# Two-sided attention on one core: six-slot bursts up to the last scores, the segment units' P @ V and the maxima's transposition later, the third octet earlier

## The chip, the cores and the metric

The kernel runs on one core of one Trainium2 chip. The metric is the device time of one execution, in microseconds (us). The engines of the core run side by side, each through its own list of instructions in order, and wait for each other by semaphores: TensorE (PE in the profile) multiplies matrices into PSUM, VectorE (DVE) and ScalarE (ACT) read PSUM, GpSimd (POOL) works on SBUF, and SyncE (SP) issues most of the DMA transfers. PSUM has eight banks of 128 partitions by 512 fp32 values, and one matrix product fills at most one bank.

## The reference

Two attentions over the same input x (2048 rows, 512 columns) are mixed by a gate, in fp32:

```python
g = sigmoid((x * gate_w).sum(-1, keepdims=True))
a = A(x)   # 32 heads of 16, softmax(q k^T / 4) v over all 2048 keys, then @ A_wo
b = B(x)   # 32 heads of 16, four segments of 512 rows:
           #   a_dot = causal softmax inside the segment, times v
           #   a_mem = (phi(q) M) / (phi(q) z + 1e-6), from the segments before
           #   o = gB * a_mem + (1 - gB) * a_dot, then @ B_wo
           #   M, z += the segment's phi(k)^T v and the sum of phi(k)
return g * a + (1 - g) * b
```

phi(t) is t + 1 for t > 0 and exp(t) otherwise; gB is the sigmoid of one number a head.

## The kernel before, in words

**Front part.** Projections of q, k and v for both sides, the gate, and B's memory terms. An fp32 value that goes into a product is split into a rounded high part and the rest (low), and three products stand for one. q and k are stored so that one product over 48 rows does all three terms of a score.

**Units and slots.** The main part is a list of units (side, g, c): four heads (group g of 8) and 512 query rows (chunk c of 4). A unit of side A has 64 slots, a unit of side B (a "segment unit") 10. One slot is one score tile: `score_part` issues the product of 128 keys by 512 queries into a PSUM bank (L661), and one exponential on ACT from there into the tile `p` (L684, L681). Four slots share a `p` tile, and there are six of these (`NP`). Units A and B alternate; the last two are B (group 7, chunk 3) and A (group 7, chunk 3). There are nS = 2368 slots in all, and the last A unit begins at slot 2304.

**Maxima ahead.** The exponent needs each row's maximum. `max_part` computes it 96 slots (`LEAD`) ahead of the scores: a product into one of four banks `sm` (L200) and a reduction on DVE (L215; L225 for the masked tiles of B). So the last 96 slots have none, and from slot 2272 on the four `sm` banks are free for other things. After a unit's last maximum, `finish_max` reduces on DVE (L178) and splits the result on POOL into `ms` (L182, L183). A number of slots later (`LATE_T` for A, four more for B) `run_late` transposes `ms` on PE into a bank `mt_ps` of the pool `st` (L191), ACT copies it to `mt` (L194), and SP writes it into two spare rows of the unit's q (L197). From then on the score product subtracts the maximum by itself. `run_late` is looked at only at the end of a burst, and takes up to two units at once.

**Bursts.** PE changes between three kinds of work: scores and maxima, P @ V, and output products. It is given them in bursts: three slots (`BURST`), then the P @ V of what is old enough. In the range `wide` (slots 2274 to 2333) a burst is six slots, the first three with the `st` banks and the next three with the free banks `sm1` to `sm3`.

**P @ V.** A piece is 128 query columns of four heads, done as four products side by side (17 columns of v each, the last one counting the sum). When a `p` tile is complete, its four pieces enter `queue` with the slot from which they may run (`GAP`, or six slots in the wide range); `some_values` joins neighbours of the same tile (L717). All go into one bank `ops`; at a unit's end ACT copies it to `oraw` (L721) and SP stores it to `od` (L722). A tile of a segment unit is first masked on POOL, by one or two `affine_select` (L665).

**Octets.** Two groups of one side make an octet of eight heads. `octet` schedules, at fixed distances in slots from t0, six steps: load (SP), factors (POOL: a reciprocal by `pow`, L776, and five small operations), send (SP: the factors to DRAM, L785), factor (SP: them back, broadcast, L789), scale (POOL, L792 to L801), store (SP, `hd`, L809). POOL and SP take these in program order, between the other things that they are given: SP the transposed maxima (L197), loads of k and v, stores; POOL the splitting of the maxima and the masks.

**Output products.** Each 128 rows of the output are 24 products (four octets, two sides, three products each, L822). Those of the chunk before are done between units. The last ones are a list `fill`, in this order: 24 for the last block of chunk 2 (bank `sm0`), 18 for block 0 of chunk 3 (`sm0` again, octets 0 to 2), and 66 for what is left except A's last octet. `load_closed` fetches the scaled octets for them (L900). In the wide range four are issued a burst, behind it two a burst of three slots. Behind the last unit's `oraw`, A's last octet is done with DVE in place of POOL, and its 12 products and the copies to the output end the kernel.

**What sets the order.** The loop at the end of `gated_mix` runs over slots n. In each it runs what is filed under `beside[n]` (octet steps, loads), then the score, the maximum of slot n + 96, and at a burst's end P @ V and either a transposition or output products.

Of the kernel before, what the change touches and what calls it, by code (L numbers as in the profile page):

```python
# [23 lines left out]
NCH = S // CH  # L24
KT = D // 128
NG = 8
# [8 lines left out]
LEAD = 96  # L35
BURST = 3
# [1 line left out]
LOW, HIGH = 6, 14  # L38
NP = 6
GAP = {"A": 2, "B": 5}  # L40
LATE_T = 8
PRE = 20
NKA, NKB = 8, 2

# [2 lines left out]
def gated_mix(ctx, tc, x, xT, wqkv, a_wo, b_wq, b_wk, b_wv, b_wo, beta, gate_w, out):  # L47
# [59 lines left out]
    end = {u: first[u] + SLOTS[u[0]] for u in units}  # L107
    seg_end = {(s, c): max(end[s, g, c] for g in range(NG)) for s in "AB" for c in range(NCH)}
    nS = len(slots)
# [4 lines left out]
    for k in range(NU):  # L114
# [4 lines left out]
        for p in range(64 + 10 * len(bs)):  # L119
            r = (len(maxs) + 1) % 2  # L120
            i = (p - start) // apart
# [42 lines left out]
    def rows(t, h, n):  # L164

        return t[64 * (h // 2):64 * (h // 2) + n, h % 2]
# [7 lines left out]
    def finish_max(u):  # L174
        nm = pmt.pop(u)
        if u[0] == "A":
            pm, nm = nm, mp.tile([128, 4, 4], F32, tag="nm", name="nm")
            nc.vector.tensor_reduce(nm, pm, axis=AX.X, op=ALU.max, negate=True)  # L178

        ms = mp.tile([128, 2, 2, 2, 4], F32R, tag="ms", name="ms")  # L180
        nv = nm.rearrange("p (r h) s -> p r h s", r=2)
        nc.gpsimd.tensor_copy(ms[:, :, 0], nv)  # L182
        nc.gpsimd.tensor_sub(ms[:, :, 1], nv, ms[:, :, 0].bitcast(F32))  # L183
        return ms
# [18 lines left out]
    def max_part(m, bank):  # L203
# [24 lines left out]
        if m == last_max[u]:  # L228
            def finish():
                late.append((m + LATE_T + (4 if side == "B" else 0), u, finish_max(u)))  # L230
            todo.append((m, finish))
# [29 lines left out]
    with ExitStack() as p0:  # L261
# [136 lines left out]
        early = vp.tile([128, NG, 4, 4, 17], F32, tag="vs", name="vs").rearrange("p g b h e -> p (g b h e)")  # L398
        early = [early[:, 1024 * i:1024 * i + 1024] for i in range(2)]
# [238 lines left out]
    stored = set()  # L638


    wide = range(nS - LEAD + 2, nS - 34)
    assert wide.start % (2 * BURST) == wide.stop % (2 * BURST) == 0

    queue = []

    def score_part(n):

        u, j = slots[n]
        side, g, c = u
        q = qt[u]  # L650

        if j % 4 == 0:
            pt_[u, j // 4] = pp.tile([128, 4, CH], F32, tag="p", name="p")
            order_p[u, j // 4] = len(order_p)
            assert not queue or order_p[queue[0][1], queue[0][2] // 4] > len(order_p) - 1 - NP
        p = pt_[u, j // 4]
        h = (0, 2, 1, 3)[j % 4]

        def score(ps, h, b, k, n0, q0):

            nc.tensor.matmul(ps[:, n0:n0 + CH - q0], rows(k[:, :, b * 128:(b + 1) * 128], h, 50),  # L661
                             rows(q[:, :, q0:], h, 50), start=True, stop=True)

        def diagonal(x):
            nc.gpsimd.affine_select(out=x, in_=x, pattern=[[0, 4], [1, 128]], base=0, channel_multiplier=-1,  # L665
                                    compare_op=ALU.is_ge, fill=0.0)

        ps = banks[1 + n % BURST] if n in wide and n // BURST % 2 else st_ps.tile([128, CH], F32, tag="st", name="st")
        if side == "A":
            score(ps, h, j // 4 % 4, kt_[u, j // 16], 0, 0)  # L670
        else:
            k = kt_[u, c]
            if j < 8:
                score(ps, h, j // 4, k, 0, 128 * (j // 4))
                if j >= 4:
                    score(ps, h, 3, k, 384, 384)
            else:
                for f in range(2):
                    score(ps, 2 * (j - 8) + f, 2, k, 256 * f, 256)
        if side == "B" and j >= 8:  # L680
            nc.scalar.activation(p[:, 2 * (j - 8):2 * (j - 8) + 2, 0:256], ps.rearrange("p (h t) -> p h t", h=2), AF.Exp,  # L681
                                 scale=SCALE)
        else:
            nc.scalar.activation(p[:, h], ps, AF.Exp, scale=SCALE)  # L684
        if j % 4 == 3 or j == SLOTS[side] - 1:
            if side == "B":
                diagonal(p[:, :, 0:128])
                if j == 7:
                    diagonal(p[:, :, 384:])
            queue.extend((n + (2 * BURST if n in wide else GAP[side]), u, i) for i in range(j // 4 * 4, j + 1))  # L690


    PIECES = ([(0, 128 * i, 128 * i) for i in range(4)] + [(1, 128 * i, 128 + 128 * i) for i in range(3)] + [(3, 384, 384)]
# [2 lines left out]
    def some_values(n, most):  # L696

        while queue and most and queue[0][0] <= n:
            _, u, i = queue.pop(0)
            most -= 1  # L700
            side, g, c = u
            w = 1
            while (queue and most and queue[0][0] <= n and queue[0][1] == u and (i + w) // 4 == i // 4
                   and (side == "A" or PIECES[i + w][0] == PIECES[i][0])):
                queue.pop(0)
                most -= 1
                w += 1
            p = pt_[u, i // 4]
            if side == "A":
                c0 = q0 = 128 * (i % 4)  # L710
                v = vt[u][:, i // 16, i // 4 % 4]
            else:
                b, c0, q0 = PIECES[i]
                v = vt[u][:, b]
            done = i + w == SLOTS[side]
            for h in range(4):
                nc.tensor.matmul(ops[32 * h:32 * h + 17, q0:q0 + 128 * w], v[:, 17 * h:17 * h + 17], p[:, h, c0:c0 + 128 * w],  # L717
                                 start=(i == 0), stop=done, tile_position=(0, 32 * h))
            if done:
                raw = ob.tile([128, CH], F32, tag="o", name="oraw")  # L720
                nc.scalar.copy(raw, ops)  # L721
                nc.sync.dma_start(od[side, c][4 * g:4 * g + 4].rearrange("h r t -> (h r) t"), raw)  # L722
                stored.add(u)
                if side == "B" and c and g % 2 == 0:
                    octet("M", g // 2, c, n + 4)
                if (side, g ^ 1, c) in stored and u != ("A", NG - 1, NCH - 1):
                    octet(side, g // 2, c, n + (20 if side == "B" and u != ("B", NG - 1, NCH - 1) else 8))
                if u in between:
                    shared.extend(output(*between[u]))
                return  # L730
# [19 lines left out]
    def octet(side, o, c, t0, vector=False):  # L750
# [6 lines left out]
        ending = o == NO - 1 and c == NCH - 1  # L757
# [51 lines left out]
                nc.sync.dma_start(hd[side, c][o], raw(k["hl"]))  # L809
                scaled.add((side, o, c))  # L810

        ts = (0, 10, 14, 18, 28, 28) if ending else (0, 10, 25, 29, 42, 54)
        for n, f in zip(ts, (load, factors, send, factor, scale, store)):
            if t0 is None:
                f()
# [3 lines left out]
    def products(ps, t, b, side, o, start, stop):  # L819

        for i, (x, w) in enumerate(((1, 0), (0, 1), (0, 0))):
            yield lambda i=i, x=x, w=w: nc.tensor.matmul(ps, t[:, b, x], wos[side][:, o, w], start=start and i == 0,  # L822
                                                         stop=stop and i == 2)
# [49 lines left out]
    last = NCH - 1  # L873
# [30 lines left out]
    def close(n, side, o, b):  # L904
        for i in range(3):
            def f(i=i):
                assert (side, o, last) in scaled
                list(products(banks[b], closed[side, o], b, side, o, (side, o) == closing[0], (side, o) == closing[-1]))[i]()
            fill.append((n, f))
    early = [(k, 0) for k in closing[:6]]  # L910
    for (side, o), b in early + [(k, b) for k in closing[:-1] for b in range(4) if (k, b) not in early]:
        close(nS - 66 if ((side, o), b) in early else max(nS - 12, end[side, 2 * o + 1, last] + 60), side, o, b)

    def jam(n):

# [5 lines left out]
    n = 0  # L921
    while n < nS or queue or beside or filled[0] < len(fill):
        for f in beside.pop(n, []):
            f()
        if n < nS:
            score_part(n)
        m = n + LEAD
        if m < nS:
            loads(m + PRE)

            max_part(m, lambda: banks[m % 4])
        run_todo(m)
        if n >= nS or n % (2 * BURST if n in wide else BURST) == (2 * BURST if n in wide else BURST) - 1:
            if shared:
                for _ in range(4):
                    shared.pop(0)()
            else:
                some_values(n, 8 if n >= nS or n in wide else MOST + jam(n))
            if n < 5:


                for i in range(4):
                    nc.tensor.matmul(ops[:, 128 * i:128 * i + 128], identf, identf, start=True, stop=True)
            if any(e[0] < m + 1 for e in late):
                run_late(st_ps, "st", m + 1)
            else:
                for _ in range(4 if n in wide else 2 if n < nS else 0 if queue else 4):
                    if filled[0] == len(fill) or fill[filled[0]][0] > n:
                        break
                    fill[filled[0]][1]()  # L950
                    filled[0] += 1
        n += 1
# [45 lines left out]
```

## Time and profile before

| | |
|---|---|
| three runs | 1836.19 us median (1835.84 to 1837.24) |
| the profiled execution | 1836.33 us, of which its span is 1834.1 us |
| PE, DVE, ACT, POOL busy | 1816.6, 1586.7, 1450.3, 605.0 us |
| mean granted TensorE clock | 0.999 |

The profile shows one execution. Its page gives each engine's busy time, the span in 40 slices, the DMA queues, the chain of work that ended last, and the costliest groups of instructions. Other views used here: the busy time of each engine in chosen stretches of the span (windows), who waited for whom (waits), and instructions in order of time, merged where neighbours are alike (timeline: start, duration, engine, line, operation, output and inputs, count, and in brackets the idle time before and what ended it). PE's matmuls overlap, so the time from one group's start to the next group's start says more than a duration. A product of fp32 operands appears as two records.

### The profile page before, as it was taken

To read this page: it belongs to the slowest core of one execution; us is meant where nothing else is said; L and a number is where in the kernel's file an instruction comes from. 1 tells how busy PE (TensorE), PEld (TensorE's weight loads), DVE (VectorE), ACT (ScalarE), POOL (GpSimd) and SP (SyncE) were. 2 spreads that over 40 slices of the span, in tenths; PEclk is the share of its full clock that TensorE was granted. 3 is DMA by queue.
4 is the path that set the end of the run, shared out by engine and by line. 5 is a ranking of instruction groups with operands and counts; after the bars stand their busy time and mean duration, and the time that the engine had idled before them with its cause. 6 is when DMAs were issued, how large, how long until landed. Compare 5 with 4: busy or idle time off the path is not lost.

```text
span 1834.1 us, 41634 instructions
## 1 busy us (share of the span) xinstructions
PE 1816.6 (99%) x15473; PEld 974.7 (53%) x15473; DVE 1586.7 (87%) x3333; ACT 1450.3 (79%) x2768; POOL 605.0 (33%) x708
## 2 busy tenths in 40 slices
PE   9999999999999999999999999999999999999998
PEld 7887766545545555444444444444444444444444
DVE  4234677999999999999999999999999999999910
ACT  5445444788888888888888888888888888888884
POOL 3001222234141414334433434342424342525351
PEclk9999999999999999999999999999999999999999
DMA  6568645433334334445454545454545444444441
GB/s 225 201 216 266 210 175 181 150 114 108 118 107 120 106 117 120 141 124 142 124 142 124 142 124 142 124 141 124 141 124 142 124 138 107 146 120 129 134 153 48
DMA packets 140617, 258.46 MB, mean 141 GB/s; under 512 B 36184, under 2 KB 60280, under 8 KB 139904
## 3 DMA queue, kind: packets, MB, share of 16 engines
q1 hardware_dynamic: 138912, 254.15, 46.7%
q8 instruction: 123, 2.02, 0.5%
q0 software_dynamic: 1216, 1.14, 0.2%
q14 instruction: 78, 0.64, 0.1%
q10 hardware_dynamic: 288, 0.52, 0.1%
HBM read 171.25 MB, written 83.25 MB: 139 GB/s over the span
## 4 chain that ended last, share of the span: by engine, by line
PE 88%; DVE 5%; POOL 2%; ACT 2%; DMA 1%; issue 1%; SPq 0%; POOLq 0%; DVEq 0%; ACTq 0%
PE ops L717 30%; PE st L661 26%; PE sm L200 13%; PE pr L298 12%; DVE pm L215 4%; PE ops L822 4%; PE sm L822 2%; POOL rcp L776 1%; DVE rest L225 1%; POOL mn L358 1%; PE num L480 1%; ACT p L684 0%; DMA raw<-xT 0%; PE mt_ps L191 0%; DMA raw<-wqkv 0%
## 5 line engine op out<-in xcount | busy, mean ns | idle before, releaser
L684 ACT ACTIVATE p<-st 128x512 f32<-128x512 f32 x2276 | 1198.6, 601 | 176.2 <-PE sm L200 118.0
L215 DVE TENSOR_REDUCE pm<-sm 128x1 f32<-128x512 f32 x2048 | 1262.1, 683 | 13.9 <-PE sm L200 13.7
L200 PE MATMUL sm<-kA,qA 48*128 48x512 f32 x2048 | 734.7, 445 | 0.0
L661 PE MATMUL st<-qA,kA 50*128 50x512 f32 x2029 | 670.2, 433 | 1.2 <-ACT mt L194 0.9
L717 PE MATMUL ops<-p,vA 128*17 128x256 f32 (+3 forms) x7440 | 560.6, 404 | 0.0
L661 PEld LDWEIGHTS st<-qA,kA 50*128 50x128 f32 x2029 | 329.8, 185 | 393.2 <-ACT p L684 332.1
L200 PEld LDWEIGHTS sm<-kA,qA 48*128 48x128 f32 x2048 | 333.6, 184 | 24.3 <-DVE pm L215 7.9
L776 POOL TENSOR_TENSOR rcp<-rec,minus 128x32 f32<-128x32 f32 x43 | 234.3, 5448 | 112.6 <-DMA rec<-dend 78.5
L717 PEld LDWEIGHTS ops<-p,vA 128*17 128x17 f32 x7440 | 153.8, 96 | 201.6 <-issue 159.4
L225 DVE CUSTOM_DVE_ANT_0 rest<-sm,mask 128x128 f32<-128x128 f32 (+3 forms) x512 | 248.6, 486 | 6.8
L665 POOL TENSOR_SCALAR_AFFINE_SELECT p<-p 128x512 f32<-128x512 f32 x128 | 79.5, 640 | 343.6 <-ACT p L684 328.3
L200 PE MATMUL sm<-kB,qB 48*128 48x128 f32 (+3 forms) x512 | 149.0, 351 | 0.0
L361 DVE TENSOR_TENSOR q<-full,q 128x512 fp32r<-128x512 f32 x64 | 44.5, 695 | 87.1 <-ACT q L354 87.1
L661 PE MATMUL st<-qB,kB 50*128 50x512 f32 (+1 forms) x495 | 109.4, 334 | 0.9 <-ACT p L684 0.8
L182 POOL CAST ms<-pm 128x16 fp32r<-128x16 f32 x32 | 6.3, 198 | 303.8 <-DVE pm L225 303.8
L661 PEld LDWEIGHTS st<-qB,kB 50*128 50x128 f32 x495 | 70.0, 185 | 61.1 <-ACT p L684 54.9
L200 PEld LDWEIGHTS sm<-kB,qB 48*128 48x128 f32 x512 | 86.9, 185 | 6.7 <-DVE pm L215 2.7
L717 PE MATMUL ops<-p,vB 128*17 128x512 f32 (+3 forms) x1024 | 87.2, 437 | 1.9 <-POOL p L665 1.9
L353 ACT COPY full<-pr 128x512 f32<-128x512 f32 x64 | 37.4, 584 | 51.1 <-PE pr L298 50.9
L358 POOL TENSOR_SCALAR mn<-full 128x512 f32<-128x512 f32 x24 | 36.3, 1512 | 102.1 <-ACT full L353 81.7
L772 DVE RECIPROCAL rec<-rec 128x32 f32<-128x32 f32 x1 | 0.4, 354 | 67.0 <-DMA rec<-odA 67.0
L298 PE MATMUL pr<-xh,wql 128*128 128x512 f32 x128 | 54.5, 426 | 1.9 <-ACT xh L411 1.7
(178 smaller groups left out, 1575.3 us busy)
## 6 DMA issues: line engine op xcount, KB each, us to landing
kA<-kdA SPq DMA_DIRECT2D x256, 128.0 KB
vA<-vdA SPq DMA_DIRECT2D x31, 544.0 KB
kA<-kdA SPq DMA_DIRECT2D x256, 64.0 KB
qdA<-q SPq DMA_DIRECT2D x32, 256.0 KB
kdA<-q SPq DMA_DIRECT2D x32, 256.0 KB
qdB<-q SPq DMA_DIRECT2D x32, 256.0 KB
qA<-qdA SPq DMA_DIRECT2D x64, 128.0 KB
kdB<-q SPq DMA_DIRECT2D x32, 256.0 KB
```

The costliest lines, as they stand in the source:

```text
L200: nc.tensor.matmul(ps[:, n0:n0 + n], rows(qt[u][:, :, s * 128:(s + 1) * 128], h, 48), rows(k[:, :, k0:k0 + n], h, 48), start=True, stop=True)
L215: nc.vector.tensor_reduce(pm[:, h, s, kc:kc + 1], ps, axis=AX.X, op=ALU.max)
L225: nc.vector.tensor_tensor_reduce(out=tri["rest"][:, 0:w], in0=ps[:, n0:n0 + w], in1=tri["mask"][:, CH - w:], scale=-1.0, scalar=3.0e38, op ...
L298: nc.tensor.matmul(ps, l(a, k), r(b, k), start=(n == 0), stop=(n == 11))
L358: nc.gpsimd.tensor_scalar_min(ph["mn"], full, 0.0)
L361: nc.vector.tensor_sub(q2, full, q1.bitcast(F32))
L661: nc.tensor.matmul(ps[:, n0:n0 + CH - q0], rows(k[:, :, b * 128:(b + 1) * 128], h, 50), rows(q[:, :, q0:], h, 50), start=True, stop=True)
L665: nc.gpsimd.affine_select(out=x, in_=x, pattern=[[0, 4], [1, 128]], base=0, channel_multiplier=-1, compare_op=ALU.is_ge, fill=0.0)
L684: nc.scalar.activation(p[:, h], ps, AF.Exp, scale=SCALE)
L717: nc.tensor.matmul(ops[32 * h:32 * h + 17, q0:q0 + 128 * w], v[:, 17 * h:17 * h + 17], p[:, h, c0:c0 + 128 * w], start=(i == 0), stop=done ...
L776: eng.tensor_tensor(r, rec, minus, op=ALU.pow)
L822: yield lambda i=i, x=x, w=w: nc.tensor.matmul(ps, t[:, b, x], wos[side][:, o, w], start=start and i == 0, stop=stop and i == 2)
```

## The change

Six edits. `LATE_T` goes from 8 to 10. The wide range ends at slot 2363 in place of 2333. In the wide range a segment unit's pieces may run after twelve slots, not six. The octets of heads 16 to 23 in chunk 3 (the third, of sides A and B and of B's memory term) get shorter distances, and B's begins 8 slots behind its unit's last P @ V, not 20. The closing products behind the first 18 may be issued from slot nS, not nS - 12. And output products come in fours wherever they come, except while P @ V is still queued behind the last slot.

```diff
-LATE_T = 8
+LATE_T = 10
...
-    wide = range(nS - LEAD + 2, nS - 34)
+    wide = range(nS - LEAD + 2, nS - 4)
...
-            queue.extend((n + (2 * BURST if n in wide else GAP[side]), u, i) for i in range(j // 4 * 4, j + 1))
+            queue.extend((n + (2 * BURST * (1 + (side == "B")) if n in wide else GAP[side]), u, i) for i in range(j // 4 * 4, j + 1))
...
-                    octet(side, g // 2, c, n + (20 if side == "B" and u != ("B", NG - 1, NCH - 1) else 8))
+                    octet(side, g // 2, c, n + (20 if side == "B" and (g < 5 or c < last) else 8))
...
-        ts = (0, 10, 14, 18, 28, 28) if ending else (0, 10, 25, 29, 42, 54)
+        ts = (0, 10, 14, 18, 28, 28) if ending else (0, 10, 18, 22, 32, 44) if (o, c) == (2, last) else (0, 10, 25, 29, 42, 54)
...
-        close(nS - 66 if ((side, o), b) in early else max(nS - 12, end[side, 2 * o + 1, last] + 60), side, o, b)
+        close(nS - 66 if ((side, o), b) in early else max(nS, end[side, 2 * o + 1, last] + 60), side, o, b)
...
-                for _ in range(4 if n in wide else 2 if n < nS else 0 if queue else 4):
+                for _ in range(0 if n >= nS and queue else 4):
```

In the program's order on each engine this moves the following. PE: 22 of the 35 transpositions stand one burst (three slots) later, and the last two become one; the other differences are behind slot 2274. There the burst of slots 2274 to 2279 gets the first four output products, the P @ V of the first segment unit stands one burst later, and so does all P @ V behind it; from slot 2334 on five bursts of six stand where ten of three were, and all 66 closing products stand behind the last P @ V, where eight of them had stood ahead of it. POOL: the scaling of B's third octet stands ahead of the splitting of the last unit's maxima and of the segment units' masks; it had stood between the masks. SP: the transfers of that octet stand some places earlier and the ones of the transposed maxima some later; B's last octet begins six slots later. DVE's order is the same.

## The prediction

> **What bounds the kernel now.** I read the chain that ended last first, then who waited for whom in the main part, then the end in order of time.
>
> ```profile
> span 1834.1 us, 41634 instructions
> ...
> PE 88%; DVE 5%; POOL 2%; ACT 2%; DMA 1%; issue 1%; SPq 0%; POOLq 0%; DVEq 0%; ACTq 0%
> ```
>
> 88% of the chain is PE. So the kernel gets shorter where PE has less to do or waits less. The profiled execution took 1836.33 us, 0.14 more than the median of the three runs; 2.2 of it lies around the span of 1834.1 and is left as it is.
>
> The waits of PE and of DVE in the stretch 600 to 1700 us (who, for whom, us in total, times, longest):
>
> ```profile
> PE mt_ps L191 <- POOL ms L183: 2.6, 3, 0.9
> DVE pm L215 <- PE sm L200: 2.5, 3, 0.8
> ```
>
> Between 600 and 1700 us PE waits for POOL three times, always at the transposition of the maxima, and DVE loses nearly as much at the same places, because its products come late. No wait of PE for a transfer is in its list there. One of the three places, PE then POOL:
>
> ```profile
> 914.43 0.38 PE L191 MATMUL mt_ps<-identf,ms 128*32 128x128 f32 x2
> 915.68 0.41 PE L191 MATMUL mt_ps<-identf,ms 128*32 128x128 f32 x2 [0.87 <-POOL ms L183]
> 916.02 0.49 PE L661 MATMUL st<-qA,kA 50*128 50x512 f32 x1
> ...
> 916.92 0.84 PE L717 MATMUL ops<-p,vA 128*17 128x384 f32 x8
> 907.97 5.43 POOL L776 TENSOR_TENSOR rcp<-rec,minus 128x32 f32<-128x32 f32 x1
> ...
> 915.41 0.22 POOL L183 TENSOR_TENSOR ms<-nm,ms 128x16 fp32r<-128x16 f32 x1
> ```
>
> The segment unit's transposition runs at 914.43, A's only at 915.68: POOL was in an octet's reciprocal (5.43 us, then its small operations) and split A's maxima at 915.41 to 915.63.
>
> In the end, a second wait for POOL: the masks of the segment units (L665) stand behind the scaling of an octet (its last operation is L801), and P @ V waits for the masks:
>
> ```profile
> 1767.57 0.63 PE L717 MATMUL ops<-p,vB 128*17 128x256 f32 x8 [1.89 <-POOL p L665]
> 1765.66 1.27 POOL L801 TENSOR_TENSOR hl<-v,hl 128x512 fp32r<-128x512 f32 x1
> 1766.88 2.99 POOL L665 TENSOR_SCALAR_AFFINE_SELECT p<-p 128x512 f32<-128x512 f32 x5
> ```
>
> And the last scores: a burst of six slots, then bursts of three, on PE.
>
> ```profile
> 1781.07 1.91 PE L717 MATMUL ops<-p,vA 128*17 128x512 f32 x16
> 1782.91 0.96 PE L822 MATMUL sm<-woB,qclosed 128*128 128x512 f32 x3
> 1783.71 0.40 PE L822 MATMUL sm<-woA,qclosed 128*128 128x512 f32 x1
> 1784.03 0.72 PE L661 MATMUL st<-qA,kA 50*128 50x512 f32 x3
> 1784.37 0.62 PE L661 MATMUL sm<-qA,kA 50*128 50x512 f32 x3
> 1784.93 1.91 PE L717 MATMUL ops<-p,vA 128*17 128x512 f32 x16
> ...
> 1803.60 0.72 PE L822 MATMUL sm<-woB,qclosed 128*128 128x512 f32 x2
> 1804.26 0.73 PE L661 MATMUL st<-qA,kA 50*128 50x512 f32 x3
> 1804.92 0.84 PE L717 MATMUL ops<-p,vA 128*17 128x384 f32 x8
> 1805.69 0.72 PE L822 MATMUL sm<-woB,qclosed 128*128 128x512 f32 x2
> ```
>
> From start to start: six scores 0.90 (1784.03 to 1784.93), eight pieces 1.84, four output products 1.12; sum 3.86 for six slots. The burst of three takes 2.09 (1803.60 to 1805.69) with two products (0.66), three scores (0.66) and three pieces (0.77). Work comes cheaper in larger groups: three and three scores cost 1.32 against 0.90 for six.
>
> What else can set the length of a burst is ACT, whose exponentials follow each other; the first row is the copy at a unit's end:
>
> ```profile
> 1776.52 0.64 ACT L721 COPY oraw<-ops 128x512 f32<-128x512 f32 x1
> 1776.99 1.66 ACT L684 ACTIVATE p<-st 128x512 f32<-128x512 f32 x3
> 1778.43 1.69 ACT L684 ACTIVATE p<-sm 128x512 f32<-128x512 f32 x3
> ```
>
> Three exponentials take 1.44, so six take 2.88 and a copy 0.47. A burst with output products is set by PE (3.86), one without by ACT (2.88 against 0.90 + 1.84 = 2.74).
>
> **Part one: the transpositions three slots later.** 22 places move behind one more burst. At the three places of the wait PE then does a burst more first. That burst lasts 0.90 (916.02 to 916.92) and some 0.84 of P @ V, so the transposition comes at about 914.43 + 1.74 = 916.17, and `ms` is ready at 915.63: the wait goes, with 0.5 to spare. What it is worth lies between nothing (DVE, also nearly full, sets the pace anyway) and 1.25 a place (915.68 - 914.43). I take DVE's own loss, 2.5 in all, since DVE cannot have it back. At the other 19 places PE waited for nothing, and the same two or four small products only stand elsewhere: 0. The cost: SP waits for `mt` about 1.7 longer at each place, and loads of k, v and octets queue behind it. They are issued 20 slots ahead, some seven bursts of over 1.7, that is 12 us; I put this at 0, with its bounds in a rival.
>
> **Part two: the end.** PE's first burst of six begins at 1751.00, the last score of all at 1810.74.
>
> ```profile
> 1751.00 0.96 PE L661 MATMUL st<-qA,kA 50*128 50x512 f32 x3
> ...
> 1810.74 0.49 PE L661 MATMUL st<-qA,kA 50*128 50x512 f32 x1
> 1811.16 1.79 PE L717 MATMUL ops<-p,vA 128*17 128x256 f32 x16
> ...
> 1813.21 2.25 PE L822 MATMUL sm<-woA,qclosed 128*128 128x512 f32 x9
> ...
> 1826.42 2.88 PE L822 MATMUL sm<-woA,hl 128*128 128x512 f32 x12
> 1824.67 0.43 DVE L801 TENSOR_TENSOR hl<-v,hl 128x256 fp32r<-128x256 f32 x1
> ```
>
> That is 59.74 before. After, each burst by the longer of PE and ACT (from slot 2274 on): six scores, four pieces (0.92), four products: 2.94. Six scores, eight pieces, the joint transposition (0.34 by 915.68 to 916.02): 3.08. Then, by what each holds: 3.35 (ACT, with a copy), 2.88 (ACT; no P @ V there now), 3.86, 3.35 (ACT, copy), 3.86, 3.82 (ACT, two copies), three of 3.86, then 3.40 with the last two products (0.90 + 1.84 + 0.66), three of 2.88 (ACT), and 1.44 for the last three slots. Sum: 52.20, or 7.54 less. The stall of 1.89 is in it: the octet's scaling now stands ahead, POOL has it done before the first mask, and P @ V comes 12 slots behind its scores. The early octet costs POOL and SP the same operations, at another time. On POOL four of them, none over L801's 1.27 by much, now stand ahead of the splitting of the last unit's maxima. If they began only at 1751.00, when those maxima are through, POOL would be done by 1751.00 + 4 x 1.3 + 0.5 = 1756.7, and the joint transposition is due at 1751.00 + 2.94 + 0.90 + 1.84 = 1756.7 too. So this costs between 0 and a few tenths; I take 0, since the scaling needs only the segment unit's maxima ahead of it, which end earlier.
>
> The last segment unit's transposition stands in the same burst as before, and its first score two bursts on, at about 1760.4 with the sums above; a copy and a transfer lie between, as before: 0. The last A unit's transposition moves from the first burst to the second, and its scores begin five bursts after the first (slot 2304): 0. The first four products move into the first burst; their operands are loaded 24 slots ahead of it: 0. The closing products behind the first 18 lose their early start, which is the 1.86 below. The six `p` tiles still suffice: a tile's exponentials need the P @ V of the sixth tile before it, and with segment pieces 12 slots late this stands at least one burst ahead in PE's order.
>
> Given back: the eight closing products that stood ahead of the last P @ V now stand behind it. 57 of them took 1813.21 to 1826.42, 0.232 each, so 1.86 more. They also cover the last unit's chain (copy, store, load, DVE, broadcast). That chain ran from 1812.95 (1811.16 + 1.79) to 1825.10 (1824.67 + 0.43), 12.15; the cover grows from 13.5 to 66 x 0.232 = 15.3, so nothing comes into view. B's last octet, six slots later, has its products last among the 66: hidden.
>
> No burst of before is six scores and eight pieces alone. From below it is ACT's 2.88, from above 3.36 (the burst of three without its products, 1.43, twice, and 0.5 for a bank that comes free late). I take 2.88, since three exponentials from `st` and three from `sm` do follow at 0.48 in the rows above; three such bursts at 3.36 would cost 1.4. As the six banks let PE run ahead of ACT over a burst's border, the sum of the longer ones can also be some 1 too much.
>
> The Trainium skill prices an exponential otherwise ("ScalarE: Activation LUTs", section "What ACT_TABLE_LOAD costs": 186 ns and 0.833 ns an element, 93 ns of it overlapping the next). By that one takes an estimated 0.52, six 3.12, and the eight bursts that ACT sets would add 1.8. The rows have 0.48, so the rows decide.
>
> **Sum.** -2.5 - 7.54 + 1.86 = -8.2. From 1836.33 that is 1828.1 for such an execution, and 1828.0 beside the median.
>
> **Rivals.**
> *The waits of the main part go, but time does not* (DVE's pace rules, or POOL's wait moves to the next transposition): 2.5 less gain, 1830.5. For it: DVE is nearly full. Against: DVE idled in the same three places.
> *Six-slot bursts without products do not pay* (ACT or the `st` banks stop PE at each border). Bursts 11 to 16 gain 22.85 - 17.34 = 5.5 (before: 1787.89 by 1784.03 + 3.86, to 1810.74); without that and without the eight products moved, 1831.7. Against: ACT's rows.
> *Slower: SP's queue.* Behind the later `mt` stand the loads of k; if one comes too late, PE's maxima stop. This decides once the 22 places lose more than 8.2 / 22 = 0.37 each; if each lost the whole 1.74, it would be 1828 + 38 = 1866. Against: no load shows as PE's wait, and 12 us of lead.
> *Slower: the clock.* In bursts without products PE idles a little each time, and the granted clock might fall. From the windows view (us, busy time and count of PE, its weight loads, DVE, ACT, POOL, clock, DMA share, GB/s):
>
> ```profile
> 1751.00:1811.20 60.20, 57.40 (x440) 24.15 (x440) 0.15 (x1) 50.12 (x100) 28.57 (x30) 1.00 0.31 103
> ```
>
> Here PE idled 2.8, 1.89 of it at once, at a clock of 1.00. At half the clock the 78 closing products would double: +18, 1846. The Trainium skill has such a fall ("TensorE: Matmul & The Clock Gate", section "A second HAM failure mode: psum-queue depth-cycling"); in this trace's end it did not happen.
> *The change does nothing that counts*: both of the first two, 1834.2.
>
> **Chances.** As worked out 0.66 (by itself 1825.5 to 1829.5); main part without gain 0.12; bursts without gain 0.08; neither 0.03; SP 0.04; clock 0.02; more than worked out (1825 or less) 0.05. The range from 1825.0 to 1832.0 takes in the first three. What a measurement can tell from no change is about 0.2%, 3.7 us, so below 1832.5 is faster: 0.87; the second rival lies near the edge and the third inside, same 0.07; slower 0.06.
>
> **What would show it.** PE's list of waits between 600 and 1700 us without `ms`; P @ V without a wait for L665 at the end; five six-slot bursts from slot 2334 on, the last three of about 2.9 with ACT full; 66 products at 0.23 behind the last P @ V, and A's last octet ready before they end. Wrong would be: PE waiting for `mt` or a load of k, a gap ahead of the last 12 products, or bursts over 3.3 without products.

## The result, and the profile after

The changed kernel takes 1827.9 us in the median (1825.46 to 1828.85), the kernel before in the runs beside it 1836.31 (1834.46 to 1838.81). The ratio is 0.9952, with a 95% interval from 0.9939 to 0.9964. The profiled execution took 1828.65, of which its span is 1826.8.

The page of the changed kernel, span and chain by engine:

```profile
span 1826.8 us, 41506 instructions
PE 94%; ACT 2%; DMA 1%; DVE 1%; POOL 1%; issue 0%; SPq 0%; POOLq 0%; DVEq 0%; ACTq 0%
```

DVE's share of the chain falls from 5% to 1%, and PE's rises from 88% to 94%. All that PE still waited for between 600 and 1700 us (DVE's list is empty), and then the first of the three old places, PE and POOL in order of time:

```profile
PE st L661 <- ACT p L684: 0.4, 2, 0.3
```

```profile
916.49 0.84 PE L717 MATMUL ops<-p,vA 128*17 128x384 f32 x8
917.14 0.39 PE L191 MATMUL mt_ps<-identf,ms 128*32 128x128 f32 x4
...
908.82 5.43 POOL L776 TENSOR_TENSOR rcp<-rec,minus 128x32 f32<-128x32 f32 x1
916.25 0.22 POOL L183 TENSOR_TENSOR ms<-nm,ms 128x16 fp32r<-128x16 f32 x1
```

POOL is in the same reciprocal, but PE does another burst first. Two units are transposed at once (four records in one group) at 917.14, and A's maxima were ready at 916.25 + 0.22 = 916.47, 0.67 earlier.

The end, PE, then POOL, ACT and DVE:

```profile
1749.14 0.99 PE L661 MATMUL st<-qA,kA 50*128 50x512 f32 x3
...
1755.05 0.39 PE L191 MATMUL mt_ps<-identf,ms 128*32 128x128 f32 x4
...
1784.28 0.72 PE L661 MATMUL st<-qA,kA 50*128 50x512 f32 x3
...
1788.14 0.72 PE L661 MATMUL st<-qA,kA 50*128 50x512 f32 x3
...
1791.55 0.72 PE L661 MATMUL st<-qA,kA 50*128 50x512 f32 x3
...
1794.29 0.73 PE L661 MATMUL st<-qA,kA 50*128 50x512 f32 x3
...
1797.45 0.72 PE L661 MATMUL st<-qA,kA 50*128 50x512 f32 x3
...
1801.56 0.49 PE L661 MATMUL st<-qA,kA 50*128 50x512 f32 x1 [0.32 <-ACT p L684]
1801.98 2.08 PE L717 MATMUL ops<-p,vA 128*17 128x512 f32 x16
...
1819.39 2.88 PE L822 MATMUL sm<-woA,hl 128*128 128x512 f32 x12
...
1751.79 1.29 POOL L801 TENSOR_TENSOR hl<-v,hl 128x512 fp32r<-128x512 f32 x1
1753.31 0.22 POOL L183 TENSOR_TENSOR ms<-nm,ms 128x16 fp32r<-128x16 f32 x1
...
1793.53 1.60 ACT L684 ACTIVATE p<-sm 128x512 f32<-128x512 f32 x3
1794.96 1.64 ACT L684 ACTIVATE p<-st 128x512 f32<-128x512 f32 x3
...
1817.83 0.42 DVE L801 TENSOR_TENSOR hl<-v,hl 128x256 fp32r<-128x256 f32 x1
```

From the first burst of six to the last score it is now 1801.56 - 1749.14 = 52.42 (before 59.74). A burst with four products takes 3.86 (1784.28 to 1788.14), the two full ones without products 2.74 and 3.16 (1791.55 to 1794.29 to 1797.45), and three of ACT's exponentials take 1.43 from start to start. PE's list of waits behind 1745 us has no L665 any more; it holds two waits of 0.3 for ACT. In the kernel before it had, beside the 1.9 for L665, one of 0.9 for ACT's copy of `mt` (L194), of which 0.3 are left. POOL scales the early octet ahead of the last maxima, which are ready at 1753.53, 1.52 before their transposition.

To compare many traces I count ACT's exponentials (L684, L681): each trace has all 2368, so the n-th in order of time marks slot n, and a stage is the time between two of them. Differences between stages are free of what happened earlier in the run. "End" is from the start of the last exponential to the end of the last copy to the output (L961). The medians and ratios (with 95% intervals) are over several runs; the kernel before ran again beside each group of kernels, and each ratio is to those runs. The three stages are from one profile of each kernel, in us.

| kernel | median us | ratio to before | slots 700 to 2250 | 2274 to last | end |
|---|---|---|---|---|---|
| before | 1836.2 to 1837.5 | 1 | 970.20 | 59.74 | 18.82 |
| changed | 1827.90 | 0.9952 [0.9939, 0.9964] | 967.57 | 52.60 | 20.78 |
| before, `LATE_T` 10 | 1833.46 | 0.9977 [0.9968, 0.9987] | 967.70 | 60.32 | 18.87 |
| changed, `LATE_T` 8 | 1835.23 | 0.9986 [0.9977, 0.9995] | 970.22 | 57.61 | 20.84 |
| the same, octet late | 1832.59 | 0.9970 [0.9961, 0.9980] | 970.44 | 53.44 | 20.81 |
| changed, octet and distance undone | 1829.93 | 0.9958 [0.9945, 0.9970] | 967.68 | 55.03 | 20.82 |
| changed, distance undone | 1830.30 | 0.9964 [0.9951, 0.9977] | 967.78 | 52.48 | 20.82 |
| changed, octet undone | 1829.43 | 0.9962 [0.9947, 0.9977] | 967.88 | 52.63 | 20.73 |
| changed, bursts of three at the end | 1832.09 | 0.9970 [0.9958, 0.9983] | 967.77 | 60.11 | 17.78 |
| changed, all products behind | 1837.30 | 1.0001 [0.9992, 1.0011] | 967.58 | 50.71 | 31.37 |
| changed, products in sixes | 1827.70 | 0.9954 [0.9941, 0.9966] | 967.91 | 54.16 | 20.74 |
| changed, `LATE_T` 13 | 1838.87 | 1.0007 [0.9998, 1.0016] | 968.42 | 62.95 | 20.84 |
| changed, `LATE_T` 16 | 1887.46 (one run) | | 1020.40 | 59.58 | 20.73 |

### The profile page after: what moved, and what is told of

Same layout as the page of the kernel before. It is cut to its first block, busy times and chain, and to the rows that moved or that the text cites. A ratio compares the mean times of both kernels' runs of the same rounds, so it can differ in the third digit from the quotient of the medians.

```text
span 1826.8 us, 41506 instructions
## 1 busy us (share of the span) xinstructions
PE 1813.5 (99%) x15409; PEld 973.1 (53%) x15409; DVE 1586.4 (87%) x3333; ACT 1448.6 (79%) x2767; POOL 604.0 (33%) x708
## 4 chain that ended last, share of the span: by engine, by line
PE 94%; ACT 2%; DMA 1%; DVE 1%; POOL 1%; issue 0%; SPq 0%; POOLq 0%; DVEq 0%; ACTq 0%
PE ops L717 32%; PE st L661 28%; PE sm L200 14%; PE pr L298 11%; PE ops L822 4%; PE sm L822 2%; ACT p L684 1%; POOL mn L358 1%; PE num L480 1%; DMA vs<-wqkv 1%; DMA raw<-xT 0%; DMA qdB<-q 0%; PE mt_ps L191 0%; PE mps L511 0%; PE sm L661 0%
## 5 line engine op out<-in xcount | busy, mean ns | idle before, releaser
L684 ACT ACTIVATE p<-st 128x512 f32<-128x512 f32 x2261 | 1191.0, 602 | 168.2 <-PE sm L200 123.0
L717 PE MATMUL ops<-p,vA 128*17 128x384 f32 (+3 forms) x7376 | 559.5, 407 | 0.0
L665 POOL TENSOR_SCALAR_AFFINE_SELECT p<-p 128x512 f32<-128x512 f32 x128 | 79.3, 637 | 336.1 <-ACT p L684 331.7
```

## The experiments

**The transpositions, alone and left out.** Theory: `LATE_T` removes three waits, worth 2.5, whatever stands at the end. Rival: no time comes of it.

```diff
-LATE_T = 8
+LATE_T = 10
```

on the kernel before:

> The kernel before with LATE_T 10 in place of 8 and nothing else. Theory (the three waits of PE for ms go, the end stays): 2.5 less than before, 1833.8 beside a median of 1836.3; in the trace no wait of PE for L183 between 600 and 1700 us, the first burst of six about 1.9 earlier than 1751.00 (as in the changed kernel, 1749.14), and from there to the last score 59.7 as before, with the wait of 1.89 for L665 still there. Rival one (waits go, time does not): 1836.3. If the end too changed, through the joint transposition of the last two units, the stretch from the first burst of six to the last score would differ from 59.7.

The stage from slot 700 to 2250 is 2.5 shorter (967.70 for 970.20), and no wait for L183 is left there, as the theory says. The rival falls. The ratio gives more, 0.9977 or 4.2 with an interval from 2.4 to 5.9; the 2.5 lies at its edge. The end got no shorter, 60.32 for 59.74: the wait for L665 is still in PE's list there, at 1.65, and behind it the granted clock falls to 0.50 for 3.4 us. PE's wait for ACT's copy of `mt` in the end does go from 0.9 to 0.3, a small gain of `LATE_T` that the prediction doesn't name.

The opposite edit on the changed kernel, `LATE_T` 8:

> The changed kernel with LATE_T 8. If the parts simply add (my prediction's sum): 2.5 more than 1827.9, so 1830.4, first burst of six at 1751.0 and the end of 52.4 as in the changed kernel. A second theory says that the parts are tied: A's last transposition is then in the first burst of six, at about 1751.0 + 0.9 + 1.0 = 1752.9, while POOL, which scales the early octet first, has ms ready only at 1753.5 + 1.9 = 1755.4; PE would wait some 2.5 there, and the time be about 1833. Rival one: 1827.9.

Here the parts do not add. The main part loses 2.65 (970.22 - 967.57), but the end loses 5.01 more, and the time is 6.2 over the changed kernel by the two ratios (0.0034 x 1836). PE's rows in order of time, and the windows view (us; busy time and count of PE, weight loads, DVE, ACT, POOL; granted clock, DMA share, GB/s) at the end of this kernel:

```profile
1755.46 0.64 PE L191 MATMUL mt_ps<-identf,ms 128*32 128x128 f32 x2 [2.17 <-POOL ms L183]
...
1757.60 3.61 PE L717 MATMUL ops<-p,vA 128*17 128x512 f32 x16
```

```profile
1753.20:1755.40 2.20, 0.09 (x4) 0.00 (x0) 0.00 (x0) 1.46 (x3) 2.04 (x4) 0.95 0.00 0
1755.40:1757.60 2.20, 2.14 (x8) 0.98 (x8) 0.00 (x0) 1.00 (x3) 0.01 (x1) 0.50 0.03 7
1757.60:1761.00 3.40, 3.40 (x19) 0.67 (x18) 0.00 (x0) 2.30 (x5) 0.00 (x0) 0.50 0.40 159
1761.00:1763.00 2.00, 2.00 (x20) 1.18 (x19) 0.00 (x0) 0.98 (x3) 0.00 (x0) 0.75 0.00 0
```

A's last maxima wait on POOL behind the octet that was moved ahead, and PE waits 2.17 for them; the second theory had 2.5. But the granted clock then falls to 0.50, and eight pieces take 3.61 in place of 1.91. How long the fall lasts can be worked out from the windows: a window lacks its length times what the clock is short of 1, and at 0.50 half is lacking, so the fall took twice the sum, 2 x (2.2 x 0.05 + 2.2 x 0.50 + 3.4 x 0.50 + 2.0 x 0.25) = 6.8 us. The second theory's 1833 had no such fall in it.

Whether it is the octet that makes this wait, the same kernel with the octet's old distances tells:

```diff
-LATE_T = 10
+LATE_T = 8
...
-... n + (20 if side == "B" and (g < 5 or c < last) else 8))
+... n + (20 if side == "B" and u != ("B", NG - 1, NCH - 1) else 8))
...
-... else (0, 10, 18, 22, 32, 44) if (o, c) == (2, last) else (0, 10, 25, 29, 42, 54)
+... else (0, 10, 25, 29, 42, 54)
```

> The changed kernel with LATE_T 8 and the third octet's old distances. If the wait of 2.17 for ms at the end of the changed kernel with LATE_T 8 alone comes from POOL scaling the early octet ahead of ms: that wait is gone here, the granted clock stays at 1.00 between slots 2274 and 2367, and the stretch from 2274 to the last exponential is about 53.5 (52.6, and 0.9 because the products start one burst later), in place of 57.6; the three waits for ms of the main part are there (2.6), time about 1831.5. If the wait comes from LATE_T alone: 57.6 again, about 1835.

The end takes 53.44, as worked out; the wait for `ms` and the fall of the clock are gone, and the main part has its old 970.44. So the early octet needs the later transposition: with `LATE_T` 8 it would have cost 57.61 - 53.44 = 4.2. The median, 1832.59, is 1.1 over the forecast and within its interval.

**The masks: octet and distance.** Both edits undone, the rest of the change kept:

> The changed kernel without the early third octet and without the longer distance of the segment units' P @ V. Theory (these two take away the wait for L665, 1.89 in the trace of before): up to 1.9 more than 1827.9, so 1829.8, with P @ V waiting for L665 again in the stretch 1749 to 1802. Rival: POOL's work is hidden anyway, since the units come at other times, 1827.9 and no wait for L665.

PE's wait at the end, and the windows view around it:

```profile
PE ops L717 <- POOL p L665: 1.6, 1, 1.6
```

```profile
1761.60:1763.30 1.70, 0.06 (x3) 0.01 (x1) 0.00 (x0) 1.70 (x5) 1.70 (x3) 1.00 0.95 355
1763.30:1765.00 1.70, 1.70 (x11) 0.98 (x12) 0.00 (x0) 1.39 (x3) 1.70 (x4) 0.61 0.80 324
1765.00:1767.00 2.00, 2.00 (x9) 1.14 (x7) 0.00 (x0) 0.14 (x1) 0.59 (x2) 0.50 0.81 311
1767.00:1769.00 2.00, 2.00 (x26) 0.60 (x24) 0.00 (x0) 2.00 (x5) 0.33 (x1) 0.98 0.74 235
```

The wait is back, so POOL's work was not hidden anyway. The end is 2.43 longer, 1.64 of wait, and behind it comes a fall of the clock for 2 x (1.7 x 0.39 + 2.0 x 0.50 + 2.0 x 0.02) = 3.4 us. The ratios (0.9958 against 0.9952) do not separate the kernels; the stage, in one profile of each, does. Then each of the two edits undone alone:

```diff
-queue.extend((n + (2 * BURST * (1 + (side == "B")) if n in wide else GAP[side]), u, i) ...
+queue.extend((n + (2 * BURST if n in wide else GAP[side]), u, i) ...
```

> The changed kernel with the segment units' P @ V six slots behind its scores, as before, and the early octet kept. Theory (the early octet alone keeps POOL free for the masks): no wait for L665 over 0.3, stretch from the exponential of slot 2274 to the last one 52.6 as in the changed kernel, time within 0.5 of it. Rival (the distance is what took the wait of 1.9 away): a wait of PE for L665 as in the kernel without both edits, 1.6 in its trace, and that stretch 55.0. The mask of a tile alone takes POOL some 0.6, which six slots (2.9 or more) cover, so I hold the theory likelier.

> The changed kernel with the third octet's old distances, and the segment units' longer distance kept. If the distance alone covers POOL's scaling between the masks (12 slots are some 6 us, the scaling takes POOL some 4.7): stretch from slot 2274 to the last exponential 52.6, no wait for L665. If the octet was what counted: wait of about 1.6 and 55.0. In the kernel without both the mask came 1.6 late, and the distance gives a burst of over 3 more, so I expect the first: either of the two edits is enough alone.

Neither has a wait for L665, and the end takes 52.48 and 52.63. PE's whole list there, the same in both, and in the changed kernel:

```profile
PE st L661 <- ACT p L684: 0.3, 1, 0.3
PE st L661 <- ACT mt L194: 0.3, 1, 0.3
```

So, by the stage, one of the two edits is enough, and both together gain no more than either. The times do not show it: with the ratios 0.9964 and 0.9962 they lie 2.2 and 1.8 over the changed kernel, where the first forecast allowed 0.5, though all these intervals overlap. In their profiles the clock fell once and twice before slot 700 (the last section), at slots where these kernels do the same work.

**The bursts of six.** The range `wide` as before, closing products allowed from nS - 12:

```diff
-    wide = range(nS - LEAD + 2, nS - 4)
+    wide = range(nS - LEAD + 2, nS - 34)
...
-        close(nS - 66 if ((side, o), b) in early else max(nS, end[side, 2 * o + 1, last] + 60), side, o, b)
+        close(nS - 66 if ((side, o), b) in early else max(nS - 12, end[side, 2 * o + 1, last] + 60), side, o, b)
```

> The changed kernel with the six-slot bursts ending at slot 2333 as before, and the eight closing products allowed ahead of slot nS again; output products stay in fours, so they can come by four in bursts of three. Theory (five six-slot bursts for ten of three gain 5.5, the eight products cost 1.86): about 3.6 more than 1827.9, so 1831.5. Rival two (six-slot bursts without products do not pay, 1831.7 had been the time for after): 1827.9 or up to 1.9 less.

The stage from 2274 is 7.51 longer, the one behind 3.00 shorter: 4.5 net in the trace, 3.3 by the ratios, where 3.6 was expected. (The two edits undone here were not undone one by one, and the fours were kept in both.) In this kernel 58 products stand ahead of the last P @ V, in the changed one 42. Its bursts of three without any product:

```profile
1788.27 0.72 PE L661 MATMUL st<-qA,kA 50*128 50x512 f32 x3
...
1789.90 1.02 PE L661 MATMUL st<-qA,kA 50*128 50x512 f32 x3
...
1795.41 0.72 PE L661 MATMUL st<-qA,kA 50*128 50x512 f32 x3
```

Four bursts of three take 1795.41 - 1788.27 = 7.14, or 3.57 for six slots; in every second one the three scores last 1.02, not 0.72. Six slots at once take 2.74 and 3.16 in the changed kernel. So bursts of six pay without products too, and rival two falls. And one line of PE's waits in this kernel:

```profile
PE sm L822 <- DVE hl L801: 0.5, 1, 0.5
```

With 16 products fewer behind the last P @ V, the last octet is no longer covered.

**No product in the bursts at all.** This asks for the prediction's unknown, the price of a burst of six without products:

```diff
-                for _ in range(0 if n >= nS and queue else 4):
+                for _ in range(0 if n < nS or queue else 4):
```

> The changed kernel with no output product ahead of the last P @ V: all 42 that stood in the six-slot bursts stand behind it. It measures the price of a burst of six without products fifteen times. With 2.88 (the prediction's value: six exponentials of 0.48, and 0.47 for each of four copies): 93 x 0.48 + 4 x 0.47 = 46.5 from the exponential of slot 2274 to the last one, some tenths more for the joint transposition, in place of 52.6; then 42 x 0.232 = 9.7 more behind it; sum 3.7 more than the changed kernel, 1831.6. With 3.36 a burst (the prediction's upper bound, late banks): 15.5 x 3.36 = 52, sum 9 more, 1837. If PE's idling in bursts without products lowered the granted clock (rival four): below 1.00 in the windows between, and more than 1837.

The time is that of the kernel before, 5.7 over the forecast of 1831.6, and as the last of the three forecasts had it. Windows view:

```profile
1756.00:1760.00 4.00, 3.35 (x21) 1.71 (x13) 0.00 (x0) 4.00 (x9) 2.39 (x4) 0.92 0.40 115
1760.00:1764.00 4.00, 4.00 (x22) 2.41 (x24) 0.00 (x0) 4.00 (x9) 1.35 (x4) 0.50 0.99 335
1764.00:1768.00 4.00, 4.00 (x36) 1.52 (x24) 0.00 (x0) 1.82 (x5) 1.20 (x3) 0.73 0.37 149
...
1776.00:1780.00 4.00, 4.00 (x19) 0.70 (x19) 0.00 (x0) 3.33 (x7) 4.00 (x1) 0.57 0.25 95
1780.00:1784.00 4.00, 4.00 (x30) 1.46 (x30) 0.00 (x0) 3.54 (x8) 1.85 (x5) 1.00 0.03 4
```

At a clock of 1.00, behind 1780, five bursts took 14.74 (scores at 1779.93 and 1794.67), 2.95 each: the 2.88 was nearly right, the bound of 3.36 far off. What the 1831.6 left out is rival four: the granted clock falls, for 6.8 and then 3.4 us (worked out as above), and the stage takes 50.71 in place of 46.5. The products behind took 10.59 more (31.37 - 20.78) where 9.7 were expected; 0.7 of that is a wait for ACT to copy a bank (L866). So products between the bursts are not only work in a good place: without them the clock fell. The runs agree with the one profile: the mean granted clock is 0.996 to 0.998 in the ten runs of this kernel and 0.999 to 1.000 in the six of the changed one. That PE is then not busy enough is the likely reason, but not shown. In the 3.41 us ahead of the first fall PE was busy for 2.76, but ahead of the second the windows view shows no idle time of PE, and the five bursts behind 1780, with the same work, kept the clock at 1.00.

**How near the later transposition is to its limit.** One and two bursts later than the change:

```diff
-LATE_T = 10
+LATE_T = 13
```

> The changed kernel with LATE_T 13: the transpositions one burst of three later again. Rival three (SP's queue) asks how near its limit lies. If one burst more costs nothing, as the first did: stretch from the exponential of slot 700 to that of slot 2250 967.6 as in the changed kernel, 52.6 from slot 2274 to the last, time 1828. If a load or the maxima themselves now come too late for the first score of a unit: waits of PE at L661 or L200 for a transfer at each unit, from some tenths to the length of a burst, 1.7, at 11 units, so up to 19 more. I expect the main part unchanged and a loss of some us at the end, where the last A unit's first score is only five bursts behind its joint transposition.

> The changed kernel with LATE_T 16: two bursts of three later than the changed kernel. If lateness is free: slots 700 to 2250 in 967.6. If rival three holds at this distance: PE waits at the first scores of units in the main part, each up to 2 x 1.7, some 10 to 40 in all, and the trace shows what it waits for (the maxima's own transfer, or a load that stood behind it on SP). Long waits of PE should also lower the granted clock to 0.50 for 3.4 us at a time, as in the kernels with waits of 1.6 to 2.2 at the end.

With 13, the main part loses 0.85 and the end 10.35. PE's transposition and wait at the end, then SP's transfers in order of time (start, duration of the issue):

```profile
1759.45 0.38 PE L191 MATMUL mt_ps<-identf,ms 128*32 128x128 f32 x2
...
1766.99 0.76 PE L661 MATMUL st<-qB,kB 50*128 50x512 f32 x1 [6.73 <-DMA qB<-mt]
```

```profile
1757.82 1.30 SPq L197 DMA_DIRECT2D qA<-mt  x2
1759.16 0.40 SPq L900 DMA_DIRECT2D qclosed<-hdB  x1
1759.61 0.43 SPq L900 DMA_DIRECT2D qclosed<-hdA  x1
1760.14 0.37 SPq L900 DMA_DIRECT2D kA<-hdB  x1
1761.18 0.32 SPq L722 DMA_DIRECT2D odA<-oraw  x1
1761.59 1.28 SPq L197 DMA_DIRECT2D qB<-mt  x2
```

and the same of the changed kernel:

```profile
1756.14 1.30 SPq L197 DMA_DIRECT2D qB<-mt  x2
...
1758.80 0.40 SPq L900 DMA_DIRECT2D qclosed<-hdB  x1
```

In the changed kernel the last segment unit's maxima went out ahead of the loads of the closing octets (512 KB each by the profile's list of transfers). With 13 the two last transpositions are apart again, A's first, and the segment unit's comes at 1759.45, so that its transfers stand behind three of those loads and a store. They are issued from 1761.59 to 1762.87, and PE's next score starts only at 1766.99, 4.1 later, after 6.73 of waiting; from 1761 to 1767 the DMA share of the windows view is 0.89 to 1.01. The granted clock falls for 13.7 us, beginning inside the wait.

With 16 the main part is hit too, at 27 places (PE's waits from 340 to 1745 us):

```profile
PE st L661 <- DMA qB<-mt: 24.2, 27, 3.2
```

The stage from slot 700 to 2250 is 52.8 longer. 23.0 of it are such waits, at 23 places, and the mean granted clock in it is 0.97: 0.03 x 1020 = 31 us of full-speed time not granted, which is most of the rest. In the end of this kernel the same three loads were out some 5 us before the maxima, the DMA share was 0.38 from 1812 to 1814, and the score started 0.8 behind the last issue, not 4.1. So rival three is real, one burst beyond the change, but it is the maxima's own transfer that is late, not a load of k behind it. That the loads hold it up with 13 is read from these two traces; no kernel moved the loads alone.

**The kernel before once more, and products in sixes.**

> The kernel before, profiled once more. In its first profile the wait of 1.89 for L665 left the granted clock at 1.00; in two kernels with the same wait at 1.65 it fell to 0.50 for 3.41 us. If the fall depends on the length of the wait alone, this profile shows 1.00 again and 59.7 from the exponential of slot 2274 to the last one. If it depends on where the wait lies in a period of 3.41 that runs by itself, the fall can be there this time (then 60.5 to 61.5), and stretches of falls can stand elsewhere, above all where segment units' narrow scores leave PE idle; each would last a multiple of 3.41.

It is the first profile again: 970.20, 59.78, the wait of 1.9, and a clock of 1.00 in the stretch. So the same wait left the clock up twice here, while behind one of 1.65 it fell in the kernel before with `LATE_T` 10, and behind one of 1.64 in the kernel without octet and distance. Its length alone does not decide. That the place in a period does is in keeping with this, but not shown.

```diff
-                for _ in range(0 if n >= nS and queue else 4):
+                for _ in range(0 if n >= nS and queue else 6):
```

> The changed kernel with output products in sixes in place of fours: the 42 products stand in seven bursts, and more bursts have none. By the prediction's prices: a burst with six products 0.90 + 1.84 + 0.2 + 6 x 0.23 = 4.32, so a pair with and without 4.32 + 2.9 = 7.2 against 2 x 3.86 = 7.72 for twelve slots with eight products in fours; per product 0.24 against 0.245 above ACT's 2.88. So some 0.5 to 1.5 less than 52.6 from slot 2274 to the last exponential, time 0.5 to 1.5 under the changed kernel. Rival: more bursts without products let the granted clock fall as in the kernel with all products behind; each fall would cost 1.2 to 1.7, and it would be no faster.

No gain: 0.9954, against 0.9952 for the changed kernel. The end took 54.16, not 51.1 to 52.1, with a new wait, behind which the clock fell for 3.4 us:

```profile
PE sm L822 <- DMA kA<-hdA: 1.3, 1, 1.3
```

The products now come before their octet is loaded. Whether sixes would pay with earlier loads wasn't tried.

## Why the prediction was right

The forecast was 1828.0, the median is 1827.9. That they agree to 0.1 is luck: the six runs spread over 3.4 us, the ratio stands for a gain of 8.8 with an interval from 6.6 to 11.2, and in the two profiles the three terms add up to 7.8 where 8.2 was forecast. The mechanism is what held. In the profiled executions the sum, by its own steps:

- *Transpositions, -2.5.* The stage gives -2.63 (970.20 to 967.57). So the time does follow the waits; whether DVE's 2.5 or PE's own 2.6 is the better measure the runs can't tell. The cover of 0.5 was 0.67 at 917.14.
- *The end, 59.74 to 52.20.* It became 52.42, -7.32. Single bursts are off, since PE runs ahead of ACT and behind it over borders (2.74, 3.16 and, with four pieces only, 2.08, where 2.88 each stood), but their sum holds.
- *Given back, +1.86.* From the last P @ V to A's last 12 products it was 15.26 and is 17.41: +2.15. The term was sized by the products alone; the last P @ V takes 2.08 for 1.79.
- *Cover of the last octet.* Its first half is ready at 1817.83 + 0.42 = 1818.25, 1.1 before the products ask for it. The kernel with 16 products fewer behind shows what that is worth.
- The rest is not the change: the main part began 0.8 later in this execution (its start lies between 328.7 and 331.5 us in the fourteen profiles), and from the last 12 products to the end it took 0.4 less. -2.63 - 7.32 + 2.15 + 0.8 - 0.4 = -7.4, the difference of the spans, which are given to a tenth (1834.1 and 1826.8).

Three steps came out right for less than their reasons, or with the reason at the wrong place:

- *The early octet at 0.* The bound put POOL's end and the joint transposition at the same 1756.7; so the 0 holds only beside the later transposition, and the sum has the two as terms that add. With `LATE_T` 8 the octet costs 4.2.
- *The stall of 1.89 as the gain of octet and distance.* Either alone removes it.
- *SP's queue at 0, by 12 us of lead for the loads of k.* The 0 held, but the margin was one burst, and at another place: the last `mt` against the loads of the closing octets. My point of decision, 0.37 at each of 22 places, was the wrong form: one burst more breaks it at one place, by 6.73, and two bursts more at 27.

*The clock* (0.02) did not fall in the changed kernel, as forecast, but the argument was thin. It rested on one trace that kept its clock through a wait of 1.89; two others with waits of 1.64 and 1.65 lost it. And bursts without products can lose it, as the rival said; the changed kernel has few of them. The page cited for it, "TensorE: Matmul & The Clock Gate" in the Trainium skill (section "A second HAM failure mode: psum-queue depth-cycling"), fits what the kernel with all products behind does: no single wait of PE over 0.5 in that stretch, and the clock falls. The other page cited from the Trainium skill, "ScalarE: Activation LUTs" (section "What ACT_TABLE_LOAD costs"), gave an estimated 0.52 an exponential. The three exponentials in 1.43 bear out 0.48, and the bursts at 2.95 without products are nearer to six of 0.48 (2.88) than to six of 0.52 (3.12).

## What to carry to other kernels

Price edits of one queue together: an octet moved ahead on one engine was free only because the work that it delayed had been moved back too. Where the last work of an in-order queue can be delayed, find what stands next to it there; the margin is the distance to that, not the general lead. And compare traces by stages between marks that both have: stages of 970 us agreed to 0.4 between kernels alike in them, where whole runs scattered by 3.

## What the runs showed of the hardware

A wait of PE can cost more than its length. Behind or inside waits of 1.3 to 6.7 us (the experiments above) the granted clock fell to 0.50, for 3.4, 6.8 or 13.7 us, always close to a multiple of 3.41; behind the wait of 1.89 it did not, in two profiles. Such falls also came in the main part, right behind a segment unit's scores, with no listed wait beside them, as in the kernel with the octet undone (windows view):

```profile
375.00:377.00 2.00, 2.00 (x13) 0.66 (x12) 2.00 (x6) 1.65 (x4) 1.75 (x3) 0.86 0.94 285
377.00:379.00 2.00, 2.00 (x11) 1.04 (x7) 1.42 (x3) 0.41 (x1) 1.92 (x4) 0.50 0.61 92
379.00:381.00 2.00, 2.00 (x23) 0.72 (x22) 1.69 (x6) 1.17 (x3) 1.82 (x2) 0.79 0.00 0
```

That is 2 x (2.0 x 0.14 + 2.0 x 0.50 + 2.0 x 0.21) = 3.4 us. From slot 0 to 700 it takes 435.3 to 435.5 in the traces without such a fall, 436.5 to 436.8 in those with one, 437.95 with two: some 1.2 each, a part of the scatter between runs. By the Trainium skill ("TensorE: Matmul & The Clock Gate", section "What's actually happening") the clock goes by a window of 3413 ns that runs by itself and by how busy PE was in it; the 3.41 here agrees. The same page of the Trainium skill advises (section "Why this matters for your kernels") to have no gaps over some 3 us; here the clock also fell behind gaps of 1.3 to 2.2.
